# Attention and a gated MLP on one core: the first loads on GpSimd's casting queue, half tiles first, values in one run, the last product in halves

## The chip, the cores and the metric

The kernel runs on one core of a Trainium2 chip. The metric is the time of one execution in device microseconds; lower is better. A core has TensorE (PE; its weight loads are listed as PEld), VectorE (DVE), ScalarE (ACT), GpSimd (POOL) and SyncE (SP), which run at the same time, each through its own list of instructions in order, and wait for one another by semaphores. Loads and stores are issued by SyncE or GpSimd and moved by 16 DMA engines.

## The reference

Sliding-window causal attention on (batch 8, heads 8, sequence 576, head size 64), window 64, and then a two-matrix MLP with SiLU on the 4608 tokens:

```python
scores = scale * q @ k^T
mask = (rel >= 0) & (rel < 64)          # rel = query position - key position
attn = softmax(where(mask, scores, -1e9))
x = (attn @ v) as [4608 tokens, 512]
h = x @ w_in                            # 512 x 2048
out = (h * sigmoid(h)) @ w_out          # 2048 x 512
```

All inputs and the output are float32; the kernel computes in bf16 with float32 sums.

## The kernel before

The sequence is cut in blocks of 64 positions, nine to a batch and 72 in all; eight blocks are a tile of 512 tokens, and there are nine tiles, j = 0 to 8.

*The order of the work* is written out by a planner (`Plan`, lines 32 to 216). Every piece of work is added with an estimated duration for each engine that may do it, its dependencies, a priority, and the PSUM banks that it takes and gives back. `run` plays this forward: whenever an engine is free, the ready piece of lowest priority number for which banks can be had goes next. The program then has that order, engine by engine. There are eight PSUM banks. `PACKET` (line 35) is the planner's estimate of the time per DMA packet by size.

*Loads.* Batch 0's q and k come on SyncE's queue as float32 (`load_first`, 538; `load_quad`, 309), two "quads" of four heads each, into space that is later used for weight sums, and are cast to bf16 by ScalarE or VectorE (`cast_quad`, 337). VectorE's stream transpose turns them into kT and qT (`turn_quad`, 340). All other inputs come on GpSimd's queue, which casts float32 to bf16 on the way (`soft`, 522): v in pairs of blocks (`load_pairs`, 560, with copies between the halves of the partitions in `place_pairs`, 574), w_in in four column ranges and two row halves (`load_w_in`, 330), w_out in eight pieces of 256 rows (`load_w_out`, 334). The string ORDER (536) sets the order of the later loads: r for batch 1's q and k, v and V for its v, w for one piece of w_out. The first 50 GpSimd loads are kept in the order in which they are added. Later batches' q and k come by head (`load_heads`, 551), their v by window (`load_windows`, 565).

*Attention* goes in visits (`visit`, 590): for one quad and a list of blocks, TensorE multiplies kT and qT into four banks (`scores`, 369), ScalarE takes the exponential (`expo`, 381), VectorE multiplies by the mask (`masking`, 384), TensorE multiplies by v in parts of three blocks, a bank for each part (`values`, 391), VectorE divides (`inverse`, `normal`) and turns the result into xt (`turn_out`, 413). Tile 0's visits are: quad 0 with all eight blocks, then quad 1 with blocks 0 to 3, then 4 to 7 (lines 839 to 841). Tile 1's are two half tiles of both quads; tiles 2 to 8 have one visit of eight blocks per quad.

*The MLP.* Tile 0 goes plainly: `plain_first` (650) has matrices of 128x128 weights against 256 tokens and SiLU on ScalarE; `plain_second` (677) runs over f, the 16 groups of 128 hidden features, in the order in which w_out lands. From tile 1 on, both products use seven products of half-size blocks instead of eight (`fast_first`, 713, and `fast_second`, 763; in the profile L475 and L487), with sums and differences of weights and tokens made by VectorE (`sum_op`, `diff_op`, lines 444 and 448; `join`, 494), copies by ScalarE (`fork`, 491), and SiLU by ScalarE (497). The results go to `ot` and are stored in two halves of the tile's rows by SyncE (501). Until the first product is issued, filler products keep TensorE busy (833).

Of the kernel before, what the change touches and what calls it, by code (L numbers as in the profile page):

```python
# [219 lines left out]
def kernel(ctx, tc, q, k, v, w_in, w_out, out):  # L220
# [83 lines left out]
    c_m = p.add({"POOL": 0.9}, const_masks, prio=-99)  # L304
# [4 lines left out]
    def load_quad(e, b, a, kk):  # L309
        dst = stage_qk[a][kk] if b == 0 else nats[b % 2][a][kk]  # L310
        queue[e].dma_start(out=dst, in_=(q, k)[kk][b, 4 * a:4 * a + 4].rearrange("h (p c) d -> (h p) (c d)", c=18))
# [22 lines left out]
    def load_w_out(e, f0, f1):  # L334
        queue[e].dma_start(out=w_out_sb[:, f0:f1], in_=w_out[128 * f0:128 * f1].rearrange("(f p) m -> p f m", p=128))

    def cast_quad(e, a, kk):
        copies[e](out=nats[0][a][kk], in_=stage_qk[a][kk])
# [82 lines left out]
    def first_plain(bank, j, fts, lo, hi):  # L421
        n = hi - lo
        for i, ft in enumerate(fts):
            for c in range(4):
                nc.tensor.matmul(
                    banks[bank.idx][:, i * n:i * n + n], lhsT=w_in_sb[:, c, 128 * ft:128 * ft + 128],
                    rhs=xts[j % NXT][:, c, lo:hi], start=(i == 0 and c == 0), stop=(c == 3), skip_group_check=True)
# [38 lines left out]
    def first_product(bank, j, u, which, start):  # L466
        a = lambda h, c: lambda z, i: w_in_sb[:, 2 * c + z, 1024 * h + 256 * u + 128 * i:1024 * h + 256 * u + 128 * i + 128]
        s = lambda n: lambda z, i: wsum1[:, n, z, 256 * u + 128 * i:256 * u + 128 * i + 128]
        b = lambda c, t: lambda z: xts[j % NXT][:, 2 * c + z, 256 * t:256 * t + 256]
        t = lambda n: lambda z: xsum[:, n, z]  # L470
        lhs, rhs = {1: (a(0, 0), b(0, 0)), 2: (a(0, 1), b(1, 0)), 3: (s(3), b(1, 1)), 4: (a(1, 1), t(3)),
                    5: (s(0), t(0)), 6: (s(1), t(1)), 7: (s(2), t(2))}[which]
        for i in range(2):
            for z in range(2):
                nc.tensor.matmul(banks[bank.idx][:, 256 * i:256 * i + 256], lhsT=lhs(z, i), rhs=rhs(z),  # L475
                                 start=(start and i == 0 and z == 0), stop=(z == 1), skip_group_check=True)

    def second_product(bank, u, pairs, which, start, stop):
# [6 lines left out]
        for i in range(2):  # L485
            for m in range(2):
                nc.tensor.matmul(banks[bank.idx][:, 256 * m:256 * m + 256], lhsT=lhs(m, i), rhs=rhs(i),  # L487
                                 start=(start and i == 0 and m == 0), stop=(stop and i == 1), skip_group_check=True)
# [47 lines left out]
    ORDER, EARLY, EP, FULL, PP = "wrvwwwwVwww", 0, 20, 4, 56  # L536

    def load_first(a):
        for kk in (1, 0):
            ld = hard(lambda e, a=a, kk=kk: load_quad(e, 0, a, kk), dma=("h4608", 128))  # L540
            ca = p.add({"ACT": 1.05, "DVE": 0.72}, lambda e, a=a, kk=kk: cast_quad(e, a, kk), [ld], -50 + a, tag="cast")
            cast_ops.append(ca)
            turn_plan(0, a, kk, 0, [ca], -50 + a)
# [16 lines left out]
    def load_pairs(b, gs):  # L560
        for g in gs:
            old = value_ops.get(b - 2, []) + [c_v[b % 2]]
            v_land[(b, g)] = soft(0.95, lambda e, g=g: load_v(e, b, g), old, dma=("s128", 1024 if g < 4 else 512), slack=SLACK * (b > 1))

# [6 lines left out]
    def place_pairs(b, g0, g1, prio):  # L571
# [9 lines left out]
        if g1 == 4:  # L581
            placed[(b, 8)].append(v_land[(b, 4)])
# [7 lines left out]
    def visit(blocks, prio, after=(), sprio=None, quads=(0, 1)):  # L590
        n, j = len(blocks), blocks[0] // 8
        exps, outs = [], []
        for a in quads:
# [15 lines left out]
            vals, norms = [], []  # L609
            for x0 in range(0, n, 3):  # L610
                part = blocks[x0:x0 + 3]
                m = len(part)
                vb = Bank("part")
                need = ma + [c_v[0], c_v[1]]
                for nb in part:
                    need = need + placed[divmod(nb, NB)]
                va = p.add({"PE": 0.02 + 0.066 * m}, lambda _, vb=vb, a=a, part=part, x0=x0: values(vb, a, part, x0), need, (prio if sprio is None else sprio) + 0.01 * a + 0.001 * x0,
                           take=[vb], tag="values")
                vals.append(va)
                for nb in part:  # L620
                    value_ops.setdefault(nb // NB, []).append(va)
# [3 lines left out]
                no = p.add({"DVE": 0.086 + 128 * m / 960}, lambda _, vb=vb, w=w, m=m, a=a, x0=x0: normal(vb, w, m, a, x0), [rc] + osb_free.get(a, []),  # L625
# [3 lines left out]
            es_free[a] = vals  # L629
# [20 lines left out]
    def plain_first(j, pieces, groups):  # L650
        done = gdone[j] = {}
        users = xt_users.setdefault(j, [])
        for k_, (lo, hi) in enumerate(pieces):
            n, size = hi - lo, groups[k_]
            for g0 in range(0, 8, size):
# [6 lines left out]
                for ft in fts:  # L662
                    need += win[ft // 2]
                op = p.add({"PE": 8 * size * mm(n)}, lambda _, bank=bank, fts=fts, lo=lo, hi=hi: first_plain(bank, j, fts, lo, hi),
                           need, 100 * j + 10 * k_ + 0.5 * g0, take=[bank], tag="first")
# [97 lines left out]
    def fast_second(j, last=False):  # L763
# [11 lines left out]
        def prod(which, bank, start, deps, k_, take=()):  # L775
            prev = None
            for u in range(4):
# [3 lines left out]
                prev = p.add({"PE": 4 * mm(256)}, lambda _, u=u: second_product(bank, u, pairs[u], which, start and u == 0, u == 3),  # L781
# [19 lines left out]
        m3 = prod(3, a, False, [fj], 0.6)  # L801
        keep_free[s] = [fj]

        def out_op(dep, bank, i, t):
            return p.add({"ACT": act(512), "DVE": dve(512)}, lambda e: fork(e, ot[:, 2 * i:2 * i + 2, 256 * t:256 * t + 256], two(at(bank))),
                         [dep] + ot_free.get((i, t), []), base + 10, give=[bank], tag="out")

        c11, c21, c12 = out_op(m2, bf, 0, 0), out_op(m4, d, 1, 0), out_op(m3, a, 0, 1)
        for i, deps in ((1, [c21, fj]), (0, [c11, c12])):
            st = p.add({"SP": 0.45}, lambda e, i=i: store(e, j, 2 * i, 2 * i + 2, 0, 512), deps, 0, dma=("h2048", 256), tag="store")  # L810
# [8 lines left out]


    load_first(0)
    load_first(1)
    load_pairs(0, range(5))
    for g in range(4):
        place_pairs(0, g, g + 1, -30 + g)
    for pi0, pi1 in ((0, 2), (2, 4), (4, 6), (6, 8)):
        for a in range(NQ):
            ld = soft(SOFT, lambda e, a=a, pi0=pi0, pi1=pi1: load_w_in(e, a, 256 * pi0, 256 * pi1), dma=("s1024", 128 * (pi1 - pi0)))
            for pi in range(pi0, pi1):
                win.setdefault(pi, []).append(ld)  # L830
# [11 lines left out]
    for what in ORDER:  # L842
        if what == "r":
            load_rows(1, 20)
        elif what == "v":
            load_pairs(1, range(3))
        elif what == "V":
            load_pairs(1, range(3, 5))
            for g in range(4):
                place_pairs(1, g, g + 1, 20 + g)  # L850
        else:
            f = len(wout)
            wout.append(soft(SOFT, lambda e, f=f: load_w_out(e, 2 * f, 2 * f + 2), dma=("s1024", 256)))
# [71 lines left out]
```

## Time and profile before

| what | us |
|---|---|
| median of 3 runs | 284.16 (284.11 to 284.2) |
| the profiled execution | 284.6 |
| its span, first to last instruction | 282.9 |
| TensorE busy | 274.3 |
| VectorE busy | 221.3 |
| ScalarE busy | 199.2 |
| GpSimd busy | 126.4 |

Times in the profile count from the start of the span; the rest of the execution, 1.7 us, lies around it. A row of a timeline has the start, the duration (of a merged group, from its first start to its last end), the engine, the source line, what is written from what, how many instructions, and in brackets the engine's idle time before and what ended it. A row of the groups has the count, the busy time, the mean duration in ns of one, and the idle time. Matmuls overlap, so their single durations are longer than the time from one to the next. A helper's line stands for all its callers. GpSimd's rows for loads are the issue, not the transfer.

### The profile page before, as it was taken

The numbers are of one execution on the slowest core, as the hardware profiler recorded it, in microseconds if no ns is written. First come the engines' busy times: TensorE is split into PE (matmuls) and PEld (weight loads), VectorE is DVE, ScalarE is ACT, GpSimd is POOL, SyncE is SP. The second block draws the span as 40 slices with busy tenths as digits, with TensorE's granted clock in tenths as the row PEclk, the third lists the DMA queues.
The fourth block names the chain that finished last, engine by engine and source line by source line (L and its number), as shares of the span: only waits on it lengthen the run. The fifth ranks groups of instructions, "written<-read, shape, count | busy, mean of one in ns | idle before, by whom it ended". The sixth has DMA issues, their size and how long they took to land.

```text
span 282.9 us, 10169 instructions
## 1 busy us (share of the span) xinstructions
PE 274.3 (97%) x4345; PEld 218.3 (77%) x4353; DVE 221.3 (78%) x501; ACT 199.2 (70%) x362; POOL 126.4 (45%) x187
## 2 busy tenths in 40 slices
PE   8999999999999999999999999999999999999993
PEld 3448844688788778887888788888887888888883
DVE  3787959999997999798959999988588848815740
ACT  4765873399859892999299946984699479528811
POOL 8455657989899789645960187000000000000000
PEclk9999999999999999999999999999999999999999
DMA  7999999999999999994999099900400040012003
GB/s 264 206 206 208 187 195 140 134 229 158 120 160 210 130 131 113 231 117 47 118 236 64 5 117 223 68 2 2 151 0 2 5 151 1 2 66 86 0 2 148
DMA packets 102093, 32.77 MB, mean 116 GB/s; under 512 B 92320, under 2 KB 96416, under 8 KB 102048
## 3 DMA queue, kind: packets, MB, share of 16 engines
q0 software_dynamic: 96576, 20.33, 81.9%
q1 hardware_dynamic: 5472, 11.80, 11.8%
q8 instruction: 34, 0.56, 0.8%
q14 instruction: 11, 0.09, 0.1%
HBM read 42.99 MB, written 9.44 MB: 185 GB/s over the span
## 4 chain that ended last, share of the span: by engine, by line
PE 49%; DMA 16%; DVE 12%; POOL 8%; ACT 7%; issue 6%; POOLq 0%; DVEq 0%; ACTq 0%
PE bank L487 26%; PE bank L475 19%; POOL nat L314 5%; DMA vv<-in_v_dram 5%; ACT g L497 5%; DMA nat<-in_q_dram 4%; DVE gsum L444 3%; DMA w_out_sb<-in_moe_w_out_dram 3%; DMA w_in_sb<-in_moe_w_in_dram 3%; DVE o L410 2%; PE bank L397 2%; PE bank L375 2%; DVE xsum L448 1%; DMA nat<-in_k_dram 1%; POOL vv L322 1%
## 5 line engine op out<-in xcount | busy, mean ns | idle before, releaser
L497 ACT ACTIVATE g<-bank 128x512 bf16<-128x512 f32 x96 | 55.4, 628 | 5.4 <-PE bank L475 5.0
L475 PEld LDWEIGHTS <-wsum 128*128 128x128 bf16 x512 | 49.4, 97 | 9.4 <-issue 2.3
L487 PEld LDWEIGHTS <-gsum 128*128 128x128 bf16 x512 | 48.0, 98 | 8.4 <-DVE gsum L444 2.4
L475 PE MATMUL bank<-xsum,wsum 128*128 128x256 bf16 x384 | 53.2, 272 | 0.6 <-DVE xsum L448 0.2
L491 ACT COPY ot<-bank 128x512 f32<-128x512 f32 x27 | 15.6, 587 | 50.1 <-PE bank L487 38.5
L487 PE MATMUL bank<-wsum,gsum 128*128 128x256 bf16 x384 | 46.9, 273 | 0.2 <-DVE gsum L444 0.2
L382 ACT ACTIVATE es<-bank 128x512 bf16<-128x512 f32 (+1 forms) x84 | 38.5, 541 | 7.4 <-PE bank L375 7.2
L475 PEld LDWEIGHTS <-w_in_sb 128*128 128x128 bf16 x384 | 37.6, 98 | 4.6
L494 DVE TENSOR_TENSOR bank<-bank,part 128x512 f32<-128x512 f32 x40 | 27.6, 691 | 16.7 <-PE bank L475 10.6
L487 PEld LDWEIGHTS <-g 128*128 128x128 bf16 x384 | 36.3, 98 | 4.8
L475 PE MATMUL bank<-xt,w_in_sb 128*128 128x256 bf16 x256 | 37.1, 273 | 0.0
L487 PE MATMUL bank<-w_out_sb,g 128*128 128x256 bf16 x256 | 34.5, 273 | 0.0
L314 POOL DMA_DIRECT2D nat<-in_k_dram x48 | 29.1, 626 | 10.8 <-DVE gsum L444 5.6
L322 POOL DMA_DIRECT2D vv<-in_v_dram x32 | 29.2, 914 | 8.4 <-PE bank L475 3.2
L444 DVE TENSOR_TENSOR gsum<-g 128x512 bf16<-128x512 bf16 x64 | 26.7, 417 | 6.1 <-ACT g L497 5.9
L314 POOL DMA_DIRECT2D nat<-in_q_dram x48 | 29.1, 622 | 4.8 <-issue 2.0
L410 DVE TENSOR_TENSOR o<-bank,rc 128x384 bf16<-128x384 f32 (+2 forms) x57 | 29.7, 522 | 1.9
L389 DVE TENSOR_TENSOR es<-es,strip 128x1024 bf16<-128x1024 bf16 (+1 forms) x42 | 24.5, 605 | 7.3 <-ACT es L382 7.2
L328 POOL DMA_DIRECT2D vv<-in_v_dram x24 | 22.1, 919 | 14.3 <-PE bank L397 13.9
L491 ACT COPY part<-bank 128x512 f32<-128x512 f32 x40 | 24.1, 603 | 4.6 <-PE bank L487 4.3
L494 DVE TENSOR_TENSOR fin<-bank,part 128x512 f32<-128x512 f32 x32 | 21.9, 684 | 5.2 <-PE bank L475 5.1
L491 ACT COPY bank<-bank 128x512 f32<-128x512 f32 x40 | 24.3, 610 | 0.2 <-DVE rc L407 0.2
(63 smaller groups left out, 387.8 us busy)
## 6 DMA issues: line engine op xcount, KB each, us to landing
out_dram<-ot SPq DMA_DIRECT2D x18, 512.0 KB, 4.2
vv<-in_v_dram POOLq DMA_DIRECT2D x56, 128.0 KB, 6.3
nat<-in_k_dram POOLq DMA_DIRECT2D x48, 72.0 KB, 4.0
nat<-in_q_dram POOLq DMA_DIRECT2D x48, 72.0 KB, 3.2
w_in_sb<-in_moe_w_in_dram POOLq DMA_DIRECT2D x8, 256.0 KB, 9.3
w_out_sb<-in_moe_w_out_dram POOLq DMA_DIRECT2D x8, 256.0 KB, 8.8
wsum<-in_k_dram SPq DMA_DIRECT2D x2, 576.0 KB, 5.1
gsum<-in_q_dram SPq DMA_DIRECT2D x2, 576.0 KB, 6.2
```

Source lines behind the costliest of these rows:

```text
L314: queue[e].dma_start(out=nats[b % 2][a][kk][32 * h:32 * h + 32].rearrange("p (n x) -> p n x", n=NB), in_=(q, k)[kk][b, 4 * a + h].rearrang ...
L322: queue[e].dma_start(out=vv[b % 2][:, :, 2 * g + 1, 0:D], in_=v[b, :, 128 * g:128 * g + 128].rearrange("h p d -> p h d"))
L328: queue[e].dma_start(out=vv[b % 2][:, :, 2 * g, 0:D], in_=v[b, :, 128 * g - 64:128 * g + 64].rearrange("h p d -> p h d"))
L382: nc.scalar.activation(out=es[a][:, h, 0:64 * n], in_=banks[bank.idx][:, 0:64 * n], func=ACTF.Exp, scale=scale)
L389: nc.vector.tensor_mul(t, t, strip[:, s:s + n].rearrange("k n i -> k (n i)").unsqueeze(1).to_broadcast([128, 2, 64 * n]))
L410: nc.vector.tensor_mul(osb[a][:, x0:x0 + n].rearrange("k n d t -> k n t d"), at_values(bank, n)[:, :, :, 0:D], rcs[w][:, 0:n].unsqueeze(3) ...
L444: (nc.vector.tensor_sub if i else nc.vector.tensor_add)(out=dst[i], in0=a, in1=b)
L475: nc.tensor.matmul(banks[bank.idx][:, 256 * i:256 * i + 256], lhsT=lhs(z, i), rhs=rhs(z), start=(start and i == 0 and z == 0), stop=(z == ...
L487: nc.tensor.matmul(banks[bank.idx][:, 256 * m:256 * m + 256], lhsT=lhs(m, i), rhs=rhs(i), start=(start and i == 0 and m == 0), stop=(stop ...
L491: copies[e](out=dst, in_=src)
L494: nc.vector.tensor_add(out=dst, in0=bank, in1=part)
L497: nc.scalar.activation(out=g_tile(pair, 256 * t, 256 * t + 256), in_=src.rearrange("k (f t) -> k f t", f=2), func=ACTF.Silu)
```

## The change

Five things change, and the planner's order follows from them.

1. Batch 0's q and k are loaded by GpSimd's casting queue, ahead of all else on it, straight into bf16; the float32 staging and the casts go. The mask constants, made by GpSimd, move behind these four loads. The order of all first loads is given by a new string: q and k of batch 0, the first two pairs of v, the first columns of w_in, and so on.
2. Tile 0's attention goes by half tiles of both quads, and the first three pairs of tile 0's first product are split in two: rows of quad 0 (c = 0, 1) and of quad 1 (c = 2, 3).
3. w_out is loaded with two neighbouring rows in each partition, so its packets are twice as long. This changes which hidden feature stands in which partition, so w_in and its sums are read with a step of two elements as TensorE's weights.
4. All values products of a visit are one piece of work: it takes its banks (three for eight blocks) at once and waits for all masks and all v of the visit.
5. In the last tile's second product, the last of the seven products, its copy and its store go by halves of the rows, and the other block of the same rows is stored by itself.

```diff
-    PACKET = {"h4608": 0.195, "h2048": 0.088, "s128": 0.0135, "s256": 0.03, "s1024": 0.081, "s2304": 0.16}
+    PACKET = {"h4608": 0.195, "h2048": 0.088, "h1024": 0.05, "s128": 0.0135, "s256": 0.03, "s1024": 0.081, "s2304": 0.16, "s2048": 0.144}
...
-    c_m = p.add({"POOL": 0.9}, const_masks, prio=-99)
+    c_m = p.add({"POOL": 0.9}, const_masks, prio=4.5)
...
     def load_w_out(e, f0, f1):
-        queue[e].dma_start(out=w_out_sb[:, f0:f1], in_=w_out[128 * f0:128 * f1].rearrange("(f p) m -> p f m", p=128))
+        queue[e].dma_start(out=w_out_sb[:, f0:f1], in_=w_out[128 * f0:128 * f1].rearrange("(p z) m -> p z m", z=f1 - f0))
...
-    def first_plain(bank, j, fts, lo, hi):
+    def first_plain(bank, j, fts, lo, hi, cs=range(4)):
...
-                    banks[bank.idx][:, i * n:i * n + n], lhsT=w_in_sb[:, c, 128 * ft:128 * ft + 128],
+                    banks[bank.idx][:, i * n:i * n + n], lhsT=w_in_sb[:, c, 256 * (ft // 2) + ft % 2:256 * (ft // 2) + 256:2],
...
-        a = lambda h, c: lambda z, i: w_in_sb[:, 2 * c + z, 1024 * h + 256 * u + 128 * i:1024 * h + 256 * u + 128 * i + 128]
-        s = lambda n: lambda z, i: wsum1[:, n, z, 256 * u + 128 * i:256 * u + 128 * i + 128]
+        a = lambda h, c: lambda z, i: w_in_sb[:, 2 * c + z, 1024 * h + 256 * u + i:1024 * h + 256 * u + 256:2]
+        s = lambda n: lambda z, i: wsum1[:, n, z, 256 * u + i:256 * u + 256:2]
...
-    ORDER, EARLY, EP, FULL, PP = "wrvwwwwVwww", 0, 20, 4, 56
+    ORDER = "q0-0 u0-2 i0-2 u2-4 i2-4 i4-6 i6-8 u4-5 o0-1 q1-1 v0-3 o1-5 v3-5 o5-8"
+    EARLY, EP, FULL, SPLIT = 0, 20, 4, 3
...
-            for x0 in range(0, n, 3):
-                part = blocks[x0:x0 + 3]
+            parts = [blocks[x0:x0 + 3] for x0 in range(0, n, 3)]
+            vbs = [Bank("part") for _ in parts]
+            need = ma + [c_v[0], c_v[1]]
+            for nb in blocks:
+                need = need + placed[divmod(nb, NB)]
+            va = p.add({"PE": 0.02 + 0.066 * n}, lambda _, vbs=vbs, a=a, parts=parts: [values(vb, a, part, 3 * i) for i, (vb, part) in enumerate(zip(vbs, parts))],
+                       need, (prio if sprio is None else sprio) + 0.01 * a, take=vbs, tag="values")
...
+                if j == 0 and k_ == 0 and g0 < SPLIT:
+                    half = [x for nb in range(4) for x in xt_done[nb][:1]] + [win[ft // 2][0] for ft in fts]
+                    op = p.add({"PE": 4 * size * mm(n)}, lambda _, bank=bank, fts=fts, lo=lo, hi=hi: first_plain(bank, j, fts, lo, hi, (0, 1)),
+                               half, 0.5 * g0, take=[bank], tag="first")
+                    first_moe.append(op)
+                    op = p.add({"PE": 4 * size * mm(n)}, lambda _, bank=bank, fts=fts, lo=lo, hi=hi: first_plain(bank, j, fts, lo, hi, (2, 3)),
+                               need + [op], 0.5 * g0, tag="first")
...
-        m3 = prod(3, a, False, [fj], 0.6)
+        m3 = [prod(3, a, False, [fj], 0.6 + 0.1 * ms[0], ms=ms) for ms in ([(0,), (1,)] if last else [(0, 1)])]
...
+        stores = [(1, (0, 2), (0, 512), [c21, fj])]
+        if last:
+            stores.append((0, (0, 2), (0, 256), [c11]))
+            for ms in range(2):
+                stores.append((0, (ms, ms + 1), (256, 512), [out_op(m3[ms], a, 0, 1, (ms,))]))
+        else:
+            stores.append((0, (0, 2), (0, 512), [c11, out_op(m3[0], a, 0, 1)]))
...
+    def load_w(what, lo, hi):
+        if what == "in":
+            for a in range(NQ):
+                ld = soft(SOFT, lambda e, a=a: load_w_in(e, a, 256 * lo, 256 * hi), dma=("s2048", 256) if hi - lo == 4 else ("s1024", 128 * (hi - lo)))
+                for pi in range(lo, hi):
+                    win.setdefault(pi, []).append(ld)
+        else:
+            for pi in range(lo, hi):
+                wout.append(soft(SOFT, lambda e, f=2 * pi: load_w_out(e, f, f + 2), dma=("s2048", 128)))
+
+    for what in ORDER.split():
+        lo, hi = [int(x) for x in what[1:].split("-")]
+        if what[0] == "q":
+            load_rows(lo, 20 if lo else -50)
+        elif what[0] in "uv":
+            load_pairs(what[0] == "v", range(lo, hi))
+            for g in range(lo, min(hi, 4)):
+                place_pairs(int(what[0] == "v"), g, g + 1, 20 + g if what[0] == "v" else -30 + g)
+        else:
+            load_w({"i": "in", "o": "out"}[what[0]], lo, hi)
...
-    visit(list(range(8)), -20, quads=(0,))
-    visit([0, 1, 2, 3], -19, quads=(1,))
-    visit([4, 5, 6, 7], -18, quads=(1,))
+    visit([0, 1, 2, 3], -20)
+    visit([4, 5, 6, 7], -18)
```

More of the change, by code (lines that the diff above doesn't have):

```diff
@@ L476, in first_product, with second_product @@
                                  start=(start and i == 0 and z == 0), stop=(z == 1), skip_group_check=True)
-    def second_product(bank, u, pairs, which, start, stop):
+    def second_product(bank, u, pairs, which, start, stop, ms=(0, 1)):
         g = lambda t, h: lambda m, i: gall[:, pairs[h], i, 256 * t + 128 * m:256 * t + 128 * m + 128]
@@ L773, in fast_second, with prod @@
         order = []
-        def prod(which, bank, start, deps, k_, take=()):
+        def prod(which, bank, start, deps, k_, take=(), ms=(0, 1)):
             prev = None
```

78 lines of the change are left out of this document (22 added, 56 removed).

## Prediction

> **What bounds the kernel now.** I read the page's busy shares first, then TensorE's timeline to see where it is dense and what it waits for, then busy time by stage, then GpSimd's queue in the first 45 us.
>
> ```profile
> PE 274.3 (97%) x4345; PEld 218.3 (77%) x4353; DVE 221.3 (78%) x501; ACT 199.2 (70%) x362; POOL 126.4 (45%) x187
> 21.27 1.04 PE L425 MATMUL bank<-xt,w_in_sb 128*128 128x256 bf16 x8
> ...
> 25.05 11.19 PE L425 MATMUL bank<-xt,w_in_sb 128*128 128x256 bf16 x101 [0.21 <-DVE xt L417]
> 36.53 2.98 PE L439 MATMUL bank<-w_out_sb,g 128*128 128x512 bf16 x12
> 39.44 0.42 PE L375 MATMUL bank<-qT,kT 32*128 32x64 bf16 x32
> ...
> 44.16 0.43 PE L397 MATMUL bank<-vv,es 128*32 128x65 bf16 x32
> ...
> 50.54 3.84 PE L439 MATMUL bank<-w_out_sb,g 128*128 128x512 bf16 x16
> 54.22 0.60 PE L475 MATMUL bank<-xt,w_in_sb 128*128 128x256 bf16 x4
> 54.66 0.60 PE L475 MATMUL bank<-xsum,wsum 128*128 128x256 bf16 x4
> ...
> 276.55 1.91 PE L487 MATMUL bank<-w_out_sb,gsum 128*128 128x256 bf16 x16
> ```
>
> Before 21.27 us TensorE's work is mostly filler. From there it is nearly dense: tile 0's first product until 36.2, its second product (L439) with tile 1's attention until 54.2, then the seven-product scheme (L475, L487) to the end. Four products of 256 columns take 54.66 - 54.22 = 0.44 us, 0.109 each. From 54.22 until the last ones end (276.55 + 1.91) there are 8 tiles x 2 products x 7 x 16 = 1792 of them by the code, 195 us of 224; the attention of seven tiles fills most of the rest. So the kernel is **TensorE-bound from 21 us on**, and the first question is when the stage at 54.2 can begin.
>
> Busy time by stage (columns: PE, PEld, DVE, ACT, POOL, then granted clock, DMA share, GB/s):
>
> ```profile
> 35.00:45.00 10.00, 9.26 (x198) 4.99 (x199) 6.23 (x19) 7.12 (x17) 5.34 (x10) 1.00 1.50 190
> 45.00:85.00 40.00, 39.37 (x688) 29.89 (x689) 39.21 (x96) 27.51 (x52) 38.15 (x61) 1.00 1.52 156
> 85.00:95.00 10.00, 9.96 (x112) 8.49 (x111) 8.39 (x18) 9.55 (x18) 8.00 (x11) 1.00 1.96 189
> ```
>
> The clock is full. VectorE is too from 45 to 85 us (39.21 of 40) and idle for 3.8 of 10 before that and 1.6 of 10 after. That is the second bound: a lead won early must pass through it.
>
> **The change, part 1: the front.** The first rows are from GpSimd's, SyncE's and ScalarE's timelines, the last from the page's DMA issues (KB each, us from issue to landing).
>
> ```profile
> 0.80 0.38 SPq L311 DMA_DIRECT2D wsum<-in_k_dram  x1
> 4.80 1.15 ACT L338 CAST nat<-wsum 128x1152 bf16<-128x1152 f32 x1 [2.73 <-DMA wsum<-in_k_dram]
> 5.79 2.12 POOL L332 DMA_DIRECT2D w_in_sb<-in_moe_w_in_dram  x3
> 10.63 0.70 POOL L332 DMA_DIRECT2D w_in_sb<-in_moe_w_in_dram  x1 [2.72 <-DMA vv<-in_v_dram]
> 11.70 0.70 POOL L332 DMA_DIRECT2D w_in_sb<-in_moe_w_in_dram  x1 [0.37 <-DMA vv<-in_v_dram]
> 24.96 0.87 POOL L322 DMA_DIRECT2D vv<-in_v_dram  x1 [0.36 <-DMA w_in_sb<-in_moe_w_in_dram]
> 35.69 0.71 POOL L335 DMA_DIRECT2D w_out_sb<-in_moe_w_out_dram  x1 [0.56 <-DMA w_out_sb<-in_moe_w_out_dram]
> nat<-in_q_dram POOLq DMA_DIRECT2D x48, 72.0 KB, 3.2
> ```
>
> GpSimd issues five v, then the eight w_in, of which three go at once. The ninth load (10.63) waits for the first v, the tenth (11.70) for the second: each waits for the one eight places before. So these waits are landing times: v's first at 10.63, one each 1.07 us, the last w_in at 24.96, the second w_out by 35.69. The five v (the fifth half as large) are in by 10.63 + 3.5 x 1.07 = 14.4, so a w_in takes (24.96 - 14.4) / 8 = 1.32 us, and 288 KB of q or k about 1.48.
>
> Removed: four ScalarE casts of 1.15 us and four SyncE loads. Added: four loads at the head of GpSimd's queue, of at most a w_in's issue each (2.12 / 3 = 0.7 us), so the v loads and the three mask instructions, which then stand behind them, move back by up to 2.8 us on GpSimd. Behind the masks wait VectorE's strip copy and the first mask multiplication, which needs scores of a q that lands after 6 us: covered; without that cover it would be those 2.8 us. The v loads lose nothing, as the DMA engines are busy with q and k until 9.5. The first k lands at 4.8 now, 4.0 after its issue. On GpSimd's queue a 72 KB load takes 3.2 in the median, so 288 KB about 3.2 + 1.1 = 4.3, and k lands at 5.1, without the cast that ends at 5.95. The four are then in by 5.1 + 3 x 1.48 = 9.5, two v by 11.7, the first two w_in by 14.3, two v by 16.5, then w_in pairs at 19.1, 21.8, 24.4.
>
> ```profile
> 11.07 1.22 DVE L348 STREAM_TRANSPOSE qT<-nat 128x576 f32<-128x576 f32 x1
> ...
> 20.24 1.03 DVE L417 STREAM_TRANSPOSE xt<-o 128x512 f32<-128x512 f32 x2
> ```
>
> The last turn of q ends at 12.3 now and at about 10.8 then (9.5 plus 1.25). With half tiles, blocks 0 to 3 need only two v: placed at 12.1, values of both quads by 13.7, division and turn by about 15.3, where the present xt is ready at 21.27. So real products start at about **15 instead of 21 us**. The first product then runs as w_in lands and is done at about 31 instead of 36.2.
>
> That lead is not kept whole. The second product goes in the order of w_out, whose second piece lands no earlier: the loads ahead of it are the same and the queue starts about 0.3 later (4.3 against 4.0), while the two w_out pieces have half the packets, whose saving no row states. I take 35.4, the present 35.69 less a small saving (bounds 34.5 to 36.5). After it 56 of 64 products are left at (54.22 - 50.54) / 17 = 0.22 us (17, since 5 of the 64 are missing in the trace), 12.3 us, and tile 1's attention. That is four times 0.42 + 0.43 and two switches of 0.1, 4.2 in all; 1.1 of it (two score groups) fits into the wait. So the stage at 54.2 starts at 35.4 + 12.3 + 3.1 = 50.8, a lead of **3.4 us**. How early the first product starts hardly matters, so SPLIT and the half products are worth nothing of their own.
>
> VectorE's full stretch is next. To run 3.4 us ahead through it, that much work must move to before 45. It has 3.8 idle there, and the masks, divisions and turns of blocks 8 to 11 can move; the weight differences cannot, as they wait for the last w_out. I take a loss of 0.6 and a gain of **2.8** (bounds 0 and 4.5).
>
> The Trainium skill ("DMA: Bandwidth & Descriptors", "Issuing engine by pattern" and "Latency and other measured facts") speaks against this move: it sends simple loads to SyncE's queue and gives a first byte at about 0.6 us there against about 1 us on GpSimd's. No row here shows both queues with one shape; with its 0.4 in place of the 0.3 from the rows, all landings and the gain of this part move by 0.1, to 2.7.
>
> **Part 2: strided weights.** Every first product now reads w_in and its sums with a step of two elements. Weight-load rows of all, then of the front:
>
> ```profile
> L475 PEld LDWEIGHTS <-w_in_sb 128*128 128x128 bf16 x384 | 37.6, 98 | 4.6
> L375 PEld LDWEIGHTS <-kT 32*128 32x128 bf16 x1152 | 10.6, 92 | 5.7 <-issue 5.7
> ...
> 10.25 0.58 PEld L375 LDWEIGHTS <-kT 32*128 32x128 bf16 x64 [0.42 <-issue]
> ```
>
> kT is already read with that step: 92 ns against 98 ns, and 64 in 0.58 us on four row groups, one per 36 ns and group. A load hides under a product of 109 ns, so I take **0**. The price comes only from 109 ns on: at twice the 98, 1024 loads would cost 87 ns each, 89 us.
>
> **Part 3: values in one run.** A visit in two runs, what stands after it on VectorE and TensorE, and the first and the last run after 54 us:
>
> ```profile
> 73.82 0.56 PE L397 MATMUL bank<-vv,es 128*32 128x65 bf16 x48
> ...
> 104.82 0.61 PE L397 MATMUL bank<-vv,es 128*32 128x65 bf16 x48
> 105.36 0.61 PE L487 MATMUL bank<-w_out_sb,g 128*128 128x256 bf16 x4
> 105.90 0.31 PE L397 MATMUL bank<-vv,es 128*32 128x65 bf16 x16
> 106.14 1.05 PE L487 MATMUL bank<-w_out_sb,g 128*128 128x256 bf16 x8
> ...
> 109.91 0.42 DVE L448 TENSOR_TENSOR xsum<-xt,xsum 128x512 bf16<-128x512 bf16 x1
> ...
> 112.67 0.60 PE L475 MATMUL bank<-xt,w_in_sb 128*128 128x256 bf16 x4
> ...
> 225.19 0.72 PE L397 MATMUL bank<-vv,es 128*32 128x65 bf16 x64
> 225.84 1.05 PE L487 MATMUL bank<-wsum,g 128*128 128x256 bf16 x8
> ```
>
> In two runs a visit costs (105.36 - 104.82) + (106.14 - 105.90) = 0.78 and two entries of 0.1 (105.90 less 105.36 less 0.44); in one (225.19 to 225.84) it costs 0.65 and one entry: 0.23 saved. The timeline has 26 such runs for the 14 visits after 54 us, so 12 go, at about 0.2: 2.4 us. Against it, one instruction group now takes three banks of eight at once and the first division waits for all blocks. Behind it on TensorE stand products of another bank, and xt waits for it. I take **1.4** (bounds -1 and 2.4).
>
> **Part 4: the end.** ScalarE's and SyncE's last rows (TensorE's is above), and GB/s in 40 slices of 270 to 283 us:
>
> ```profile
> 276.75 0.58 ACT L491 COPY ot<-bank 128x512 f32<-128x512 f32 x1 [2.86 <-PE bank L487]
> 277.36 2.12 SPq L501 DMA_DIRECT2D out_dram<-ot  x2
> 278.50 0.58 ACT L491 COPY ot<-bank 128x512 f32<-128x512 f32 x1 [1.16 <-PE bank L487]
> ...
> GB/s 0 0 0 0 0 0 0 0 0 0 50 0 0 0 0 0 0 0 0 0 0 0 0 0 0 227 397 384 372 233 69 391 391 391 359 13 0 0 0 0
> ```
>
> The last 512 KB move in four slices of 0.325, 1.3 us. With halves the last copy has 256 columns, about 0.3 instead of 0.58, and the last store a quarter of the bytes, about 0.35 instead of 1.3: 0.25 + 0.95 = **1.2 us**. Two more stores of 0.4 us issue go earlier on SyncE. If they queue behind the other 512 KB (moving until 279.7), 0.3 is left; with all of it, 1.5.
>
> **Sum.** 2.8 + 0 + 1.4 + 1.2 = 5.4 us. The profiled execution took 284.6 (span 282.9 and 1.7 around it), so 279.2; the median of the three runs, 284.16, is 0.44 lower, so **278.8**.
>
> **Rivals.** *The lead is absorbed.* VectorE's 39.21 of 40 speaks for it, the idle 3.8 us before and the later slack against. The front then brings 0.3, the runs 0.7, the end 1.2: 282.0. That the change doesn't bring products forward at all has the same time. *Everything holds:* 4.5 + 2.4 + 1.5 = 8.4, 275.8. *Slower: the three banks.* While the scheme holds three and the next scores four, a visit gets no three; the sums of xt end at 110.33 and the next tile's products start at 112.67, so it decides from 2.3 us later on. At 3.3 TensorE waits 1 us at each of seven tiles, and the runs' 1.4 turn into 7 lost: 284.16 - 2.8 - 1.2 + 7 = 287.2. For it: eight banks are all there are. Against: the run of 64 at 225.19 already stands in the present kernel, and the product behind it starts at once. *Slower: strided weights,* some 370.
>
> **Chances.** Forecast (276.8 to 281) 0.50; everything holds 0.11; absorbed 0.24; within 0.2%, about what a measurement here can tell from no change, 0.03; slower 0.12 (banks 0.09, weights 0.03). Faster is the first three, 0.85. The range from 275.8 to 283.8 takes in the bounds of the front and of the runs and the absorbed case, and leaves out the slower ones.
>
> **What would show it.** The first L425 near 15 us and no ScalarE cast; the first L475 near 50.8; the weight loads of L475 still near 98 ns and 0.44 us for four products; 14 value runs after the first L475; last store of a quarter size. The forecast is wrong if the second w_out lands late, if VectorE makes TensorE wait between 50 and 85, or if products wait for xt.

## The result and the profile after

The changed kernel takes **288.88 us** (median of four runs, 288.3 to 289.03) against 284.13 of the kernel before: ratio 1.0164 [1.0146, 1.0182]. It is slower, and the forecast of 278.8 (275.8 to 283.8) is wrong by ten microseconds. The profiled execution took 288.74, its span is 287.0.

In the changed kernel the helpers' lines are: first product of tile 0 L421 (before L425), second L435 (L439), values L393 (L397), the seven-product scheme L471 and L483 (L475 and L487), turn into xt L413 (L417), copies L487 (L491), the loads of w_in L331 and of w_out L334.

From the page of the changed kernel: span, busy shares, the clock in 40 slices, and the weight loads of the scheme's first product.

```profile
span 287.0 us, 10148 instructions
...
PE 269.6 (94%) x4330; PEld 217.4 (76%) x4330; DVE 220.2 (77%) x505; ACT 195.8 (68%) x364; POOL 127.6 (44%) x191
...
PEclk9975999999999999999999999999999999999999
...
L471 PEld LDWEIGHTS <-w_in_sb 128*128 128x128 bf16 x384 | 37.6, 98 | 4.7
```

TensorE is busy for 4.7 us less than before (269.6 us against 274.3) in a longer span. Fewer fillers run, 11.5 us against 17.2, so its own work is about the same and the loss is idle time; the clock row points to the first 30 us. Its timeline there and, last, one of the value runs:

```profile
15.55 0.27 PE L421 MATMUL bank<-xt,w_in_sb 128*128 128x256 bf16 x1
24.32 0.80 PE L421 MATMUL bank<-xt,w_in_sb 128*128 128x256 bf16 x3 [8.50 <-DMA w_in_sb<-in_moe_w_in_dram]
25.05 0.63 PE L393 MATMUL bank<-vv,es 128*32 128x65 bf16 x32
...
33.06 9.44 PE L421 MATMUL bank<-xt,w_in_sb 128*128 128x256 bf16 x85 [0.55 <-DVE xt L413]
...
60.47 0.60 PE L471 MATMUL bank<-xt,w_in_sb 128*128 128x256 bf16 x4
...
225.60 0.72 PE L393 MATMUL bank<-vv,es 128*32 128x65 bf16 x64
```

The first real product starts at 15.55, as forecast. The second waits 8.50 us for a load of w_in, and the values, scores and products behind it in TensorE's order wait with it. Which load is it? GpSimd's queue tells when each had landed, since each load waits for the one eight places before:

```profile
14.19 0.70 POOL L331 DMA_DIRECT2D w_in_sb<-in_moe_w_in_dram  x1 [1.30 <-DMA w_in_sb<-in_moe_w_in_dram]
15.48 0.71 POOL L331 DMA_DIRECT2D w_in_sb<-in_moe_w_in_dram  x1 [0.59 <-DMA w_in_sb<-in_moe_w_in_dram]
...
24.47 0.89 POOL L321 DMA_DIRECT2D vv<-in_v_dram  x1 [0.79 <-DMA w_in_sb<-in_moe_w_in_dram]
```

These are the 15th, 16th and 23rd loads, so they mark the 7th, 8th and 15th: the first, second and seventh piece of w_in. The data of the waiting product (c = 1, columns 0 to 255) are in the first piece, landed by 14.19. TensorE starts again at 24.32, when the **seventh** lands: same rows, but columns 1536 to 2047, which the product doesn't read. Busy time by stage (columns as before):

```profile
15.00:20.00 5.00, 0.76 (x4) 0.10 (x1) 1.72 (x6) 2.18 (x5) 2.48 (x4) 0.82 1.52 196
20.00:25.00 5.00, 0.68 (x3) 0.29 (x3) 0.00 (x0) 0.00 (x0) 2.12 (x4) 0.50 1.32 202
25.00:30.00 5.00, 5.00 (x119) 3.76 (x119) 3.65 (x12) 3.36 (x7) 3.22 (x5) 0.65 1.12 212
...
45.00:85.00 40.00, 39.56 (x727) 27.77 (x725) 37.11 (x94) 28.04 (x58) 36.21 (x58) 1.00 1.48 148
85.00:95.00 10.00, 9.17 (x142) 7.95 (x141) 9.12 (x19) 6.79 (x12) 10.00 (x14) 1.00 1.59 159
```

All compute engines stand from 20 us until that landing, and the clock is at half there and at 0.65 in the next stretch. Later, VectorE is no longer full (37.11 of 40). The end, from TensorE's and ScalarE's timelines, first the start of tile 8:

```profile
258.11 0.60 PE L471 MATMUL bank<-xt,w_in_sb 128*128 128x256 bf16 x4
...
281.20 1.26 PE L483 MATMUL bank<-w_out_sb,gsum 128*128 128x256 bf16 x10
282.50 0.37 ACT L487 COPY ot<-bank 128x256 f32<-128x256 f32 x1 [0.51 <-PE bank L483]
282.92 0.82 PE L483 MATMUL bank<-w_out_sb,gsum 128*128 128x256 bf16 x6 [0.46 <-ACT ot L487]
283.77 0.37 ACT L487 COPY ot<-bank 128x256 f32<-128x256 f32 x1 [0.90 <-PE bank L483]
```

The span divides by two marks, the first products of the scheme in tile 1 and in tile 8. Before, the second mark is

```profile
253.46 0.60 PE L475 MATMUL bank<-xt,w_in_sb 128*128 128x256 bf16 x4
```

| us | before | after | difference |
|---|---|---|---|
| start to tile 1 | 54.22 | 60.47 | +6.25 |
| tile 1 to tile 8 | 199.24 | 197.64 | -1.60 |
| tile 8 to the end of the span | 29.44 | 28.89 | -0.55 |
| span | 282.9 | 287.0 | +4.1 |

The runs and the end bring 2.15 us; the front loses 6.25 where 3.4 were to be won.

### The profile page after: what moved, and what is told of

Read it like the earlier page. It is cut to its first block, busy times and chain, and to the rows that moved or that the text cites. A ratio compares the mean times of both kernels' runs of the same rounds, so it can differ in the third digit from the quotient of the medians.

```text
span 287.0 us, 10148 instructions
## 1 busy us (share of the span) xinstructions
PE 269.6 (94%) x4330; PEld 217.4 (76%) x4330; DVE 220.2 (77%) x505; ACT 195.8 (68%) x364; POOL 127.6 (44%) x191
## 3 DMA queue, kind: packets, MB, share of 16 engines
q1 hardware_dynamic: 5184, 9.44, 9.3%
HBM read 42.99 MB, written 9.44 MB: 183 GB/s over the span
## 4 chain that ended last, share of the span: by engine, by line
PE 61%; ACT 12%; DVE 11%; DMA 8%; issue 5%; POOL 3%; DVEq 0%; ACTq 0%; POOLq 0%
PE bank L483 29%; PE bank L471 22%; DMA w_in_sb<-in_moe_w_in_dram 6%; ACT g L493 5%; PE bank L421 5%; PE bank L393 3%; PE bank L371 3%; DVE gsum L440 3%; ACT es L378 2%; DVE o L406 2%; DVE es L385 1%; ACT bank L487 1%; DMA vv<-in_v_dram 1%; ACT part L487 1%; POOL vv L321 1%
## 5 line engine op out<-in xcount | busy, mean ns | idle before, releaser
L493 ACT ACTIVATE g<-bank 128x512 bf16<-128x512 f32 x96 | 56.0, 622 | 5.2 <-PE bank L471 4.6
L471 PEld LDWEIGHTS <-wsum 128*128 128x128 bf16 x512 | 49.7, 98 | 8.3 <-issue 0.8
L483 PEld LDWEIGHTS <-gsum 128*128 128x128 bf16 x512 | 48.0, 98 | 8.8 <-DVE gsum L440 1.4
L471 PE MATMUL bank<-xsum,wsum 128*128 128x256 bf16 x384 | 53.5, 272 | 0.3 <-DVE bank L490 0.3
L483 PE MATMUL bank<-wsum,gsum 128*128 128x256 bf16 x384 | 47.2, 273 | 0.5 <-DVE bank L490 0.3
L487 ACT COPY ot<-bank 128x512 f32<-128x512 f32 (+1 forms) x27 | 15.2, 572 | 41.8 <-PE bank L483 28.0
L471 PEld LDWEIGHTS <-w_in_sb 128*128 128x128 bf16 x384 | 37.6, 98 | 4.7
L483 PEld LDWEIGHTS <-g 128*128 128x128 bf16 x384 | 37.0, 98 | 4.5
L490 DVE TENSOR_TENSOR bank<-bank,part 128x512 f32<-128x512 f32 x40 | 27.6, 693 | 15.5 <-PE bank L471 10.0
L471 PE MATMUL bank<-xt,w_in_sb 128*128 128x256 bf16 x256 | 37.4, 273 | 0.0
L321 POOL DMA_DIRECT2D vv<-in_v_dram x32 | 30.1, 941 | 9.4 <-PE bank L393 7.2
L483 PE MATMUL bank<-w_out_sb,g 128*128 128x256 bf16 x256 | 33.9, 273 | 0.0
L327 POOL DMA_DIRECT2D vv<-in_v_dram x24 | 22.8, 950 | 16.5 <-PE bank L393 16.5
L385 DVE TENSOR_TENSOR es<-es,strip 128x1024 bf16<-128x1024 bf16 (+1 forms) x44 | 25.1, 586 | 6.6 <-ACT es L378 5.7
L487 ACT COPY part<-bank 128x512 f32<-128x512 f32 x40 | 24.1, 602 | 5.0 <-PE bank L483 5.0
L487 ACT COPY bank<-bank 128x512 f32<-128x512 f32 x40 | 24.2, 605 | 1.5 <-PE bank L471 1.2
```

Of the source, the lines that this page charges most:

```text
L321: queue[e].dma_start(out=vv[b % 2][:, :, 2 * g + 1, 0:D], in_=v[b, :, 128 * g:128 * g + 128].rearrange("h p d -> p h d"))
L327: queue[e].dma_start(out=vv[b % 2][:, :, 2 * g, 0:D], in_=v[b, :, 128 * g - 64:128 * g + 64].rearrange("h p d -> p h d"))
L385: nc.vector.tensor_mul(t, t, strip[:, s:s + n].rearrange("k n i -> k (n i)").unsqueeze(1).to_broadcast([128, 2, 64 * n]))
L487: copies[e](out=dst, in_=src)
L490: nc.vector.tensor_add(out=dst, in0=bank, in1=part)
L493: nc.scalar.activation(out=g_tile(pair, 256 * t, 256 * t + 256), in_=src.rearrange("k (f t) -> k f t", f=2), func=ACTF.Silu)
```

## The experiments

**Theory.** The step of two elements makes a product wait for loads that it doesn't need. The instructions of the changed program, as compiled, show the waits of the first four weight loads:

```
c=0: L421 Ldweights w_in_sb [waits DMASW6_49]
c=1: L421 Ldweights w_in_sb [waits DMASW6_49,DMASW4_49,DMASW2_49]
c=2: L421 Ldweights w_in_sb [waits DMASW7_49]
c=3: L421 Ldweights w_in_sb [waits DMASW7_49,DMASW5_49,DMASW3_49]
```

With contiguous weights each waits for one. A piece of w_in covers two rows (c = 0, 1 or 2, 3) and 512 columns; in a partition's memory the rows lie 2048 elements apart. From its first to its last element, a piece of later columns spans the start of the second row: exactly the view for which the program waits for the three later pieces, and not the first row's. So the waits fit a bookkeeping that compares contiguous boxes exactly and a stepped view by such a span. **Rivals:** reading with a step is itself slow; the three banks, or the new queue for q and k, cost the time.

**1. Plain weights.** The changed kernel with w_out's old layout, and so contiguous weights; all else stays.

```diff
-        ... w_out[...].rearrange("(p z) m -> p z m", z=f1 - f0)
+        ... w_out[...].rearrange("(f p) m -> p f m", p=128)
-        lhsT=w_in_sb[:, c, 256 * (ft // 2) + ft % 2:256 * (ft // 2) + 256:2]
+        lhsT=w_in_sb[:, c, 128 * ft:128 * ft + 128]
...
```

> Part 3 of the change alone undone: w_out's rows and the weights' columns as before, all else as changed. Theory: in the changed kernel the second strided weight load of the first product waits for all three later column ranges of its row half (TensorE idle from 15.8 to 24.3 us), because the strided view counts as overlapping them. Without the stride the wait is for its own load only; the first product of tile 1 starts at 51 to 53 us instead of 60.5, and the time falls by 7 to 10 us to 279 to 282. Rival (the half tiles in TensorE's fixed order are what blocks it, by v or by w_in that really is late): the time stays above 286.

Measured: **281.79 us**, 0.9917 [0.9896, 0.9938] of before. TensorE's timeline:

```profile
16.36 0.60 PE L421 MATMUL bank<-xt,w_in_sb 128*128 128x256 bf16 x4
...
18.05 0.30 PE L371 MATMUL bank<-qT,kT 32*128 32x64 bf16 x15 [0.49 <-issue]
...
19.50 3.26 PE L421 MATMUL bank<-xt,w_in_sb 128*128 128x256 bf16 x24
...
25.15 9.44 PE L421 MATMUL bank<-xt,w_in_sb 128*128 128x256 bf16 x85 [0.21 <-DVE xt L413]
...
34.88 2.03 PE L435 MATMUL bank<-w_out_sb,g 128*128 128x512 bf16 x8
37.17 1.24 PE L435 MATMUL bank<-w_out_sb,g 128*128 128x512 bf16 x5 [0.26 <-DMA w_out_sb<-in_moe_w_out_dram]
...
53.78 0.60 PE L471 MATMUL bank<-xt,w_in_sb 128*128 128x256 bf16 x4
```

The wait is gone, and 7.1 us with it (288.88 - 281.79). But tile 1 starts only 0.44 us before the kernel before, where the forecast had 3.4; of that below.

**2. The step kept, the waits gone.** w_in in four tiles of 512 columns and its sums in four of 256, so that no piece's span covers another's; the longer packets stay.

```diff
-    w_in_sb = keep.tile([128, 4, d_ff], BF16, name="w_in_sb")
+    w_in_ts = [keep.tile([128, 4, 512], BF16, name=f"w_in_sb{i}") for i in range(4)]
-    wsum1 = keep.tile([128, 4, 2, 1024], BF16, name="wsum1")
+    wsum1 = [keep.tile([128, 4, 2, 256], BF16, name=f"wsum1{i}") for i in range(4)]
```

> The changed kernel with the stride kept, but w_in in four tiles by column range and the sums of w_in in four tiles, so that a strided view can't overlap another range's load. Theory: the same gain as without the stride, and a little more by w_out's longer packets: 278.5 to 281.5. Rival (reading weights with a step of two is itself slow): weight loads over 98 ns, four products over 0.44 us, and a time like the changed kernel's, 288 to 289. Rival (the order blocks): above 286.

Measured: 282.12 us, 0.9919 [0.9904, 0.9933]. TensorE's timeline (the lines stand three earlier here):

```profile
15.32 0.60 PE L418 MATMUL bank<-xt,w_in_sb 128*128 128x256 bf16 x4
...
54.27 0.60 PE L468 MATMUL bank<-xt,w_in_sb 128*128 128x256 bf16 x4
54.71 0.60 PE L468 MATMUL bank<-xsum,wsum 128*128 128x256 bf16 x4
```

Four stepped products still take 0.44 us, and the time is that of plain weights. With the mean of 98 ns above, slow reading falls: it was the waits. The longer packets bring nothing that these runs can tell; in this trace the granted clock is 0.76 from 20 to 25 us, where experiment 1 has 1.00, so a small gain could be hidden by that.

**3. The step alone**, in the kernel before (the lines of the first diff the other way round).

> The kernel before with only w_out's longer packets and the strided weights. Theory: its first product (21.3 us) would now wait for the last w_in of each row half (23.7 and 25.0 us), so TensorE loses about 3 us there: 286.5 to 288. Rival (the stride costs nothing and the wait belongs to the new order): 284, less what the packets save.

Measured: 286.93 us, 1.0091 [1.0076, 1.0106]. TensorE's timeline of this kernel:

```profile
21.26 0.27 PE L425 MATMUL bank<-xt,w_in_sb 128*128 128x256 bf16 x1
23.32 0.38 PE L425 MATMUL bank<-xt,w_in_sb 128*128 128x256 bf16 x2 [1.79 <-issue]
24.51 0.71 PE L425 MATMUL bank<-xt,w_in_sb 128*128 128x256 bf16 x5 [0.81 <-DMA w_in_sb<-in_moe_w_in_dram]
```

The waits are for the same later pieces: the one for the first row half ends at 23.32, one for the second at 24.51. In the changed kernel the first of them ended at 24.32. But here the first product stands at 21.26 instead of 15.55, so the waits are short, 1.79 and 0.81 us. The step's price depends on how early the products come: 2.6 us here, 7.1 in the changed kernel. The earlier first product made it dearer.

**4. The wait filled.** The changed kernel with 40 filler products ahead of the first half product, into the bank that it then overwrites: the wait stays, the idle time goes.

```diff
+                        for _i in range(40 if g0 == 0 else 0):
+                            nc.tensor.matmul(banks[bank.idx], lhsT=fill[:, 0:128], rhs=fill, start=True, stop=True)
```

> The changed kernel with 40 filler products (512 columns each, results overwritten) put before the first half product, so that the wait stays and the clock is kept up. Theory: the wait is the cost and the lowered clock (0.50 to 0.65 from 20 to 30 us) a small part: 1 to 2 us less than the changed kernel, 287 to 288. Rival (the lowered clock is the main cost): 4 us or more less, 285 or below.

Measured: 287.85 us, 1.0121 [1.0105, 1.0136]. TensorE's timeline:

```profile
15.83 8.80 PE L657 MATMUL bank<-fill 128*128 128x512 bf16 x40
24.46 0.60 PE L421 MATMUL bank<-xt,w_in_sb 128*128 128x256 bf16 x4
```

The wait is full of fillers, and the first product starts where the second did after the gap. The same kernel's busy time by stage:

```profile
25.00:30.00 5.00, 4.93 (x137) 3.62 (x137) 3.71 (x12) 4.14 (x9) 3.28 (x5) 1.00 1.12 211
```

The clock is full in this stretch, where it was 0.65, and the time 1.0 us less (0.6 by the two spans, 286.4 and 287.0). So of the step's 7.1 us about one at most is the lowered clock, the rest the wait.

**5 and 6. Values in one run.** First plain weights (experiment 1) with the values in parts again, the code of before; then the kernel before with the values in one run and nothing else.

```diff
-            va = p.add({"PE": 0.02 + 0.066 * n}, ..., take=vbs, tag="values")
+            for x0 in range(0, n, 3):
+                va = p.add({"PE": 0.02 + 0.066 * m}, ..., take=[vb], tag="values")
```

> Plain weights as in the first experiment, and the values products again in parts of three blocks (part 3 of the prediction undone). The stretch from the first to the last tile's first product was 199.2 us before and 197.4 us with single runs. Theory: the single runs save those 1.8 us, so this takes 283.0 to 284.0. Rival (three banks at once cost what the switches save, and the gain came from elsewhere): 281.8, no change.

Measured: 286.33 us, 1.0095 [1.0062, 1.0127]: 4.5 us above plain weights, outside what either theory gave. In TensorE's timeline the scores of the second half tile are broken by a wait, and the first products behind it are slow:

```profile
18.05 0.30 PE L371 MATMUL bank<-qT,kT 32*128 32x64 bf16 x16 [1.21 <-issue]
...
19.65 4.45 PE L421 MATMUL bank<-xt,w_in_sb 128*128 128x256 bf16 x24 [0.68 <-ACT es L378]
```

and in the same kernel's busy time by stage the clock (after the POOL column) is low again:

```profile
20.00:25.00 5.00, 5.00 (x61) 3.66 (x59) 1.56 (x6) 3.97 (x7) 2.01 (x4) 0.66 1.33 201
```

Tile 1 starts 1.56 us later than with single runs, and from tile 1 to tile 8 it takes 2.54 us more. The second figure fits the parts: TensorE's timeline has 26 value runs behind tile 1's first product and 14 in experiment 1, and twelve at the 0.2 us of the prediction are 2.4. The first is in the main the clock's: the wait in the scores ends at 18.05 in experiment 1 too, and the 24 products take 4.45 us here and 3.26 there, 1.2 of the 1.56. That the parts lower the clock isn't shown; experiment 2, with single runs, has 0.76 in the same stretch.

> The kernel before with nothing but the values products of a visit in one run. Theory: fewer switches save 1.6 to 2.4 us between the first and the last tile: 282.0 to 282.8. Rival (three banks at once): 284.4 or more. Rival (what the run with parts lost, 4.5 us, is what single runs give): 280.

Measured: 283.5 us, 0.9962 [0.9948, 0.9975], 0.8 us less than the kernel before measured beside it (284.31). Tile 1 to tile 8 takes 198.22 us, 1.02 less than before, tile 1 starts 0.06 later. The gain is there, but below the 1.6 to 2.4 of the theory. Once in the stretch, TensorE waits for the sums of xt:

```profile
85.49 1.03 PE L475 MATMUL bank<-xsum,wsum 128*128 128x256 bf16 x8 [1.40 <-DVE xsum L448]
```

In the kernel before, this wait is 0.25 us. So the runs give what was reckoned, and about half of it goes to that wait. The rival of the three banks, 1 us of waiting at each of seven tiles, isn't seen: there is one such wait, and the stretch gets shorter.

**7. The end whole**, on plain weights.

```diff
-        m3 = [... for ms in ([(0,), (1,)] if last else [(0, 1)])]
+        m3 = [... for ms in [(0, 1)]]
-        if last:
+        if False:
```

> Plain weights, and the last product, its copy and its store whole again. With halves TensorE's last six products wait 0.46 us for ScalarE's copy out of the same bank. Theory: the halves gain 0.5 us net instead of the forecast 1.2, so this takes 282.1 to 282.5. Rival (the wait eats the gain): 281.8 or less. Rival (the forecast): 283.0.

Measured: 282.76 us, 0.9948 [0.993, 0.9966], between the theory's 282.5 and the forecast's 283.0. The medians, which lie 1.0 apart with runs from 282.32 to 284.7 us, don't decide; the two profiled spans differ by 0.6 (280.7 and 280.1). From TensorE's end to the span's end, halves take 3.27 us, the whole 4.68; from tile 8 to TensorE's end, halves take 25.63, the whole 25.01. Halves win 1.4 behind TensorE and give 0.6 back in it, at the wait of 0.46 shown above.

**8. q and k on SyncE**, with the casts, on plain weights; the order of the rest is that of the changed kernel.

```diff
-            load_rows(lo, 20 if lo else -50)
+            if lo:
+                load_rows(lo, 20)
+            else:
+                load_first(0)
+                load_first(1)
...
```

> Plain weights, and batch 0's q and k again on SyncE's queue with casts on ScalarE or VectorE; the new order of the other loads, half tiles, single runs and halves stay. Theory: GpSimd's queue carries q and k first, so the second w_out lands 1.5 us later than before (37.2 against 35.7) and tile 1 starts only 0.4 us earlier; with SyncE's queue working beside it the loads land earlier: 280.5 to 281.5. Rival (the casts and the shared start cost as much as they give): 281.8 or more, up to 283.

Measured: 282.25 us, 0.9927 [0.9914, 0.994], which can't be told from plain weights; I had expected less. The load that waits for the second piece of w_out, in GpSimd's timeline, here and (second row) in experiment 1:

```profile
35.94 0.71 POOL L335 DMA_DIRECT2D w_out_sb<-in_moe_w_out_dram  x1 [0.54 <-DMA w_out_sb<-in_moe_w_out_dram]
37.41 0.71 POOL L334 DMA_DIRECT2D w_out_sb<-in_moe_w_out_dram  x1 [0.55 <-DMA w_out_sb<-in_moe_w_out_dram]
```

The piece lands 1.5 us earlier here. The first product starts at 16.80 here and at 16.36 there, tile 1 at 53.23 and 53.78, and from tile 1 to tile 8 it takes 198.32 here and 197.42 there: what is won in front is lost behind. The new queue brings nothing by itself.

**9. Tile 0 as before**, on plain weights: its three visits and whole first products.

```diff
-    EARLY, EP, FULL, SPLIT = 0, 20, 4, 3
+    EARLY, EP, FULL, SPLIT = 0, 20, 4, 0
-    visit([0, 1, 2, 3], -20)
-    visit([4, 5, 6, 7], -18)
+    visit(list(range(8)), -20, quads=(0,))
+    visit([0, 1, 2, 3], -19, quads=(1,))
+    visit([4, 5, 6, 7], -18, quads=(1,))
```

> Plain weights, and tile 0's visits as before (quad 0 with all eight blocks first) with the half products undone; q and k on GpSimd's queue. Theory: how early the first product starts hardly matters, as w_out's landing sets the second product: 281.5 to 283. Rival (the half tiles carry the front's gain): TensorE starts 4 us later and most of it stays, 284 to 286.

Measured: 285.76 us, 1.0059 [1.0037, 1.008]. TensorE's timeline, the first product of tile 0:

```profile
23.91 1.36 PE L421 MATMUL bank<-xt,w_in_sb 128*128 128x256 bf16 x11
25.48 12.93 PE L421 MATMUL bank<-xt,w_in_sb 128*128 128x256 bf16 x117 [0.21 <-DVE xt L413]
...
56.30 0.60 PE L471 MATMUL bank<-xt,w_in_sb 128*128 128x256 bf16 x4
...
120.60 0.24 PE L393 MATMUL bank<-vv,es 128*32 128x65 bf16 x8 [1.03 <-DMA vv<-in_v_dram]
122.28 0.24 PE L393 MATMUL bank<-vv,es 128*32 128x65 bf16 x8 [1.43 <-DMA vv<-in_v_dram]
```

The first product starts 7.6 us later than with half tiles and ends at 38.41 instead of 34.59; tile 1 starts at 56.3 instead of 53.78, 2.5 us later. The profiled execution (287.37 us) also has 2.5 us of waits for v near 120 us, which are not part of the front. With this order of loads the half tiles carry the front, against what I had predicted of them. But the order is made for half tiles: two of the four v pairs of tile 0 go behind the first w_in, and a visit of eight blocks waits for all four. The first product starts 2.6 us later than even in the kernel before (21.27), whose loads begin with all v. Whole visits with such an order, beside the rest of the change, weren't tried, so how much of the 2.5 us is the half tiles' own stays open.

**10. The loads in another order**, on plain weights: all v of tile 0 first, three pieces of w_out ahead of batch 1's q and k.

```diff
-    ORDER = "q0-0 u0-2 i0-2 u2-4 i2-4 i4-6 i6-8 u4-5 o0-1 q1-1 v0-3 o1-5 v3-5 o5-8"
+    ORDER = "q0-0 u0-4 i0-2 i2-4 i4-6 i6-8 u4-5 o0-3 q1-1 v0-3 o3-5 v3-5 o5-8"
```

> Plain weights, and another order of the first loads: all four v pairs ahead of w_in, and three pieces of w_out ahead of batch 1's q and k. With plain weights alone the second half tile's xt came at 25.1 us, TensorE then had 85 of 128 products left, and the second w_out landed at 37.2. Theory: these two set the start of tile 1; with both earlier tile 1 starts at 51.5 to 53 instead of 53.8, and the time falls to 280 to 281.3. Rival (batch 1's attention, now later, takes their place): 53.8 or later, 281.8 or more.

Measured: **280.54 us**, 0.9879 [0.9845, 0.9914]. TensorE's timeline:

```profile
15.52 0.60 PE L421 MATMUL bank<-xt,w_in_sb 128*128 128x256 bf16 x4
...
23.87 9.44 PE L421 MATMUL bank<-xt,w_in_sb 128*128 128x256 bf16 x85 [0.56 <-DVE xt L413]
...
33.81 3.84 PE L435 MATMUL bank<-w_out_sb,g 128*128 128x512 bf16 x16
...
51.03 0.60 PE L471 MATMUL bank<-xt,w_in_sb 128*128 128x256 bf16 x4
```

The second half's xt comes 1.3 us earlier than in experiment 1 and the second product runs without a wait for w_out. Tile 1 starts at 51.03 us, near the 50.8 of the forecast. This version beats both kernels.

## Why the prediction was wrong

**Strided weights, the step that failed.** "A load hides under a product of 109 ns, so I take 0." The price per load was right (98 ns, 0.44 us for four). But I asked only what a stepped read costs, not what it waits for. The rows that I took the price from couldn't show a wait: batch 0's kT gets its data from one instruction per quad, w_in from eight loads that land one after the other. The step cost 7.1 us through dependences on loads whose data it doesn't touch, shown by taking away either the step (experiment 1) or the shared tile (experiment 2). The rival named for it, slow loads at some 370 us, was another mechanism. That the dependences come from comparing spans is inferred from which loads are waited for.

**The front.** First product: 15 forecast, 15.55 measured, and by the way that was forecast: in VectorE's timeline the last turn of q ends at 11.1 (10.8 forecast) and the first xt at 15.5 (15.3). Without the step, several numbers behind it were off. The first product was to end "at about 31"; in experiment 1 it ends at 34.59. Half tiles bring only the first half forward: the second half's xt is as late as before (25.15 against 25.05), with 85 recorded products, 9.44 us, still to run. The second piece of w_out was to land at 35.4 (34.5 to 36.5); TensorE waits for it until 37.17 in experiment 1 (in the changed kernel a load behind it in the queue waits for it until 37.07), outside the bounds, and experiment 8 shows where 1.5 us of that comes from: with q and k in the same queue, the loads behind them go out later. That "the queue starts about 0.3 later" was too little. From the landing to tile 1 experiment 1 takes 16.6 us where 12.3 + 3.1 were forecast: only one of the two score groups fitted in ahead of it, and TensorE stood for 0.59 in the middle of another. And "How early the first product starts hardly matters" is wrong in this order of loads: without the visits by halves and the half products the first product ends at 38.41, after that landing, and decides (experiment 9). What SPLIT and the half products are worth alone wasn't tested. With both landings mended, tile 1 starts 3.2 us earlier (experiment 10), the size that I forecast.

**VectorE.** A loss of 0.6 was set aside. From tile 1 to tile 8 experiment 10 takes 198.20 us and experiment 1, which starts 2.75 later, 197.42. Experiment 8, which starts 0.55 earlier than experiment 1, takes 198.32. That fits a loss of 0.8 to 0.9, but no run separates VectorE from other causes.

**Values in one run.** Forecast 1.4 (-1 to 2.4). Twelve runs go, 14 instead of 26, as forecast. Alone this brings 0.8 in the medians and 1.0 from tile 1 to tile 8, with 1.40 us of waiting for the sums of xt against it, the loss that the 1.4 allowed for; in the changed kernel's surroundings it brings 2.5 there. The mechanism was right, the size within the bounds but for the last figure.

**The end.** Forecast 1.2 (0.3 to 1.5): from TensorE's end to the span's it is 1.2 (4.44 before, 3.26 after), but TensorE itself ends 0.6 later for it. 0.55 is left. The missed term is the second half's wait for the copy of the first out of the same bank.

**What it adds up to.** Plain weights bring 0.44 + 1.82 + 0.54 = 2.8 us of span by the marks of the table; the step turns this into a loss of 4.1.

## What to carry to other kernels

When an edit changes the shape of a view that an engine reads, ask not only how long the read takes but which writes it is now thought to overlap; look at the waits of the first instructions that use it, and keep pieces that land at different times in tiles of their own. A false wait costs little while something else is late anyway (2.6 us in the kernel before) and becomes dear when another part of the same change brings its reader forward. Bringing half of a tile's work forward moves the end of a stage only if what the other half and the next stage wait for moves too.

## What the runs showed of the hardware

**The clock.** TensorE's granted clock was 0.50 from 20 to 25 us and 0.65 from 25 to 30, behind the gap of 8.50 us; with fillers in the gap it was 1.00. By finer stretches it fell 2.4 us after the last product (15.55 + 0.27 = 15.82) and came back at 28.5. Two rows of the changed kernel, then two of experiment 5 (columns as before):

```profile
15.90:18.20 2.30, 0.00 (x0) 0.00 (x0) 0.86 (x3) 0.73 (x2) 0.77 (x2) 1.00 1.42 198
18.25:28.45 10.20, 4.13 (x107) 2.69 (x108) 2.23 (x7) 3.16 (x7) 6.03 (x10) 0.50 1.24 206
16.57:19.98 3.41, 1.45 (x76) 1.12 (x69) 2.77 (x10) 2.19 (x6) 1.91 (x3) 1.00 1.28 203
20.00:23.40 3.40, 3.40 (x19) 2.42 (x17) 1.11 (x4) 3.20 (x6) 1.25 (x3) 0.50 1.24 206
```

The Trainium skill ("TensorE: Matmul & The Clock Gate", "Part 1: The HAM clock gate (the "warmup" mystery)") gives half rate after an idle window of about 3.4 us. The trace agrees with the half rate, but TensorE wasn't idle for that long: 2.4 us in the changed kernel, and in experiment 5 a stretch in which it was busy for 1.45 of 3.41 us and no wait was longer than 1.21. So a stretch that is only partly idle was enough here; how much of it must be idle is open.

**Halves of a bank.** The second half of the last product writes other columns of the bank than those being copied out. Its first two products run ahead of the copy, and the other six start only when the copy is done, by a semaphore (0.46 us idle). The Trainium skill ("PSUM — Partial Sum Buffer", "PSUM bank collisions raise a hardware error") says to guard by bank and group of 32 partitions, or more simply by bank, and not by address; the copy here covers all 128 partitions, and the trace agrees with a wait kept by bank. Two banks for the two halves would avoid it; that wasn't tried.
